# New due times in the first w_in stage, another chain first in the later ones, and separate banks for the last product

## The chip, the cores and the metric

The kernel runs on one core of one Trainium2 chip. The metric is device time in microseconds (us). TensorE is written PE, VectorE DVE, ScalarE ACT, GpSimd POOL, SyncE SP. SBUF is the on-chip memory, PSUM the banks that matrix products are written to. Weights of a product are loaded by a row of their own, PEld.

## The reference

Two operators, one after the other: softmax attention over 8 batches, 12 heads, 448 tokens of 64 elements, and on its result a feed-forward layer with a leaky ReLU.

```python
scores = q @ k.transpose(0, 1, 3, 2) / sqrt(64)
attn = exp(scores - max(scores)); attn = attn / (sum(attn) + 1e-9)
x = (attn @ v).transpose(0, 2, 1, 3).reshape(3584, 768)
h = x @ w_in                      # 768 -> 2048
out = maximum(0.01 * h, h) @ w_out   # 2048 -> 768
```

All inputs and the output are float32; the kernel computes in bfloat16 with float32 sums in PSUM.

## The kernel before

**Units.** Two heads of one batch are a unit; there are 48, in order of batch, and they are written u. For each unit the kernel loads q, k and v (`load_soft`, line 153, by DMAs that POOL issues), casts them (`cast`, line 183, on POOL: L190 for q and k, L198 to L203 for v), transposes q and k (on TensorE as L303 with a VectorE copy L307 for the first 15 units, by SP's DMA afterwards, L276 and L285), computes scores (L321, later L324), exponentials on ScalarE (L333, L336, L338), the weighted sum with v (L364, later L345 and L352), and divides by the row sums on VectorE (a reciprocal L974 and a product L975). The result x is transposed into xT, by SP's DMA or, for three units named in `X_PE`, on TensorE (L391, with a VectorE copy L392).

**Stages.** The tokens are cut into seven stages of 640, 512, 512, 512, 512, 384 and 512. In each stage x is multiplied with w_in, ScalarE applies the leaky ReLU, and the result h is multiplied with w_out; attention for later tokens runs between these products, so that TensorE always has work. Stage 0 is different: its w_in products run in `head` (448 tokens, L426) and `neck` (192 tokens, L814) while w_out is still loading. Stages 1 to 6 use `hidden` for w_in and `second`, which calls `block_pair`, for w_out.

**Seven products for eight.** Both matrix products are split into two halves in three directions and use seven half-size products with sums and differences of operands (Strassen's scheme in Winograd's form). The sums of the weights are made once on VectorE (`mix_w_in`, `mix_weights` with L438, L440, L443, L447, `mix_deep`); those of x and h for each stage (L501, L597, L522 and L523).

**PSUM.** Eight banks are used: two single ones, `banks` (g0, g1), and three pairs, `slots` (sc0 to sc2), each with two banks. In attention a slot takes a pair of scores, a weighted sum, or an x transpose. A bank or slot can be written again when its last reader on ScalarE or VectorE is done.

**w_in stages.** `hidden(i)` works through the hidden columns in two rounds (r) of two groups each. One group's seven products use the two banks, the other's use the first banks of two slots; these are the two chains, `chains = [banks, slots]`. The loop takes one product of each chain in turn, the banks' chain first (x = 0), then the slots' chain (x = 1). Each product is six matmuls (L550). Between rounds the two banks of each chain change places. From stage 2 on a product of the preceding stage's last w_out quarter (`deep`, L646) follows each pair. The stage before ends in `late()` of `block_pair` with a product into each of the two `banks` (L683), read by VectorE in `join` (L694): two reads of the bank b, one of the bank a.

**First stage, planned.** `place` (line 1069) decides in stage 0 what attention work goes between the w_in products. It keeps a model of the time: `model["now"]` for TensorE, `model["act"]` for ScalarE, `free` for the time at which a slot can be written, `ready` for the time at which a unit's exponentials are there, and `owed_x` for x transposes on TensorE, which are due 2.0 after the weighted sum in the model. With `lazy` the last one or two exponentials of a burst of three are emitted later, after the next leaky ReLU (`late`, `settle`). Everything is a fixed order of instructions when the program is built; nothing is decided on the chip.

**POOL's order.** `feed(g)` follows each burst: it casts the next unit (`cast`), then calls `fetch`, which issues loads up to the unit `ahead`. `FAR` is unit 16; from burst 12 on `ahead` is at least FAR.

**The end.** `closing` is the last part of the last stage. One product goes into bank b; ScalarE copies it to the right half of o2 (L733), VectorE adds it to the left half (`join`), and the left half is stored. Then come four products of 192 columns (eight matmuls each, L683): two with the right halves' common operand, into bank a and a slot's bank; VectorE adds each to o2 (L741); and two more that add onto the same two banks, after which VectorE adds the sums to o1. Stores are issued by SP and ScalarE, one part each (L404).

Of the kernel before, what the change touches and what calls it, by code (L numbers as in the profile page):

```python
# [16 lines left out]
def kernel(  # L17
# [9 lines left out]
    nc = tc.nc  # L27
# [6 lines left out]
    NSC = S // SC  # L34
    KD = DM // P
    MD = DF // P
    NW = DM // 2
# [75 lines left out]
    w_out_sb = w_pool.tile([P, MD, DM], BF16)  # L113
# [396 lines left out]
    def token(i, x):  # L510

        return KEEP * P if x == KEEP else cuts[i] + x * P
# [12 lines left out]
    def hidden(i):  # L525

        n = cuts[i + 1] - cuts[i]
        nh = n // 2
        at = place_of(cuts[i])
        near, far = slice(0, KH), slice(KH, KD)  # L530
        one, two = slice(at, at + nh), slice(at + nh, at + n)
        t2, t3, t4 = (x_mix[:, x, :, :nh] for x in range(3))
        hs = h[:, :, spots(i)[0] * P:spots(i)[0] * P + n]
        taken = [next_slot() for _ in range(2)]
        del slots[1:]
        chains = [banks, [x[:, 0] for x in taken]]

        def act(m, cols, x):
            nc.scalar.activation(  # L539
                hs[:, m:m + 2, cols], x.rearrange("p (m t) -> p m t", m=2), AX.Prelu, alpha=0.01  # L540
            )

        def group(chain, m):
            b, a = (x[:, :2 * nh] for x in chain)
            left, right = slice(0, nh), slice(nh, n)

            def product(ps, w, x, first=False):
                for j in range(2):
                    for kk in range(KH):
                        nc.tensor.matmul(  # L550
                            ps[:, j * nh:(j + 1) * nh], w[:, kk, ts(j, P)], x[:, kk],
                            start=(first and j == 0 and kk == 0), stop=(kk == KH - 1), skip_group_check=True,
                        )

            def fresh():
                return c_pool.tile([P, 4 * P], F32, name="c")[:, :2 * nh]

            cl, ch = slice(m * P, (m + 2) * P), slice(FH + m * P, FH + (m + 2) * P)
            s2, s3, s4 = (w_in_mix[:, x, :, cl] for x in range(3))
            product(b, w_in_sb[:, near, cl], xT[:, near, one], first=True)  # L560
            c11 = fresh()
            nc.scalar.copy(c11, b)
            yield
            product(a, w_in_sb[:, far, cl], xT[:, far, one], first=True)
            nc.vector.tensor_add(c11, c11, a)  # L565
            yield
            product(b, s2, t2)
            act(m, left, c11)
            c12 = fresh()
            nc.scalar.copy(c12, b)  # L570
            yield
            product(a, w_in_sb[:, near, ch], xT[:, near, two], first=True)
            c22 = fresh()
            nc.scalar.copy(c22, a)
            yield
            product(b, s3, t3)
            nc.vector.tensor_add(c22, c22, b)
            yield
            product(a, s4, xT[:, far, two])
            nc.vector.tensor_add(c12, c12, a)  # L580
            act(MH + m, right, c22)
            yield
            product(b, w_in_sb[:, far, ch], t4)
            act(m, right, c12)
            act(MH + m, left, b)
            yield

        ready = []
        more = deep(i - 1) if i > 1 else None
        for r in range(2):  # L590
            ms = [4 * r, 4 * r + 2]
            todo = [group(chains[x], ms[x]) for x in range(2)]
            for step in range(7):
                for x in range(2):
                    yield
                    if r == 0 and step == 2 and x:
                        nc.vector.tensor_sub(t4, xT[:, far, one], t2)  # L597
                    next(todo[x])
                    if i > 1 and (r or step) and x == 1:
                        next(more, None)  # L600
                    if step == 2 and ready:
                        mix_h(i, ready.pop(0))
            for c in chains:
                c.reverse()
            ready += ms
        slots.extend(taken)
        for m in ready:
            mix_h(i, m)
# [52 lines left out]
    def block_pair(i, c):  # L661
# [31 lines left out]
        def join(o, at, ps):  # L693
            nc.vector.tensor_add(o[:, at], o[:, at], ps[:, :NW])  # L694
# [34 lines left out]
        def closing():  # L729

            both = (nc.sync, nc.scalar)
            yield from product(b, s3, t3)
            idle(o2[:, right], b[:, :NW])  # L733
            join(o2, left, b)
            store(o2, t0, left, both)
            yield
            pieces = [(ps, ts(x, QW), slice(NW + x * QW, NW + (x + 1) * QW)) for x, ps in enumerate((a, slots[0][:, 0]))]
            for o, y, w, first in ((o2, h[:, lo, two], t1, True), (o1, h[:, hi, one], w_out_sb[:, hi, right], False)):
                for ps, cols, at in pieces:
                    yield from product(ps, y, w[:, :, cols], first=first, cols=cols)  # L740
                    nc.vector.tensor_add(o[:, at], o[:, at], ps[:, cols])  # L741
                    if o is o1:
                        store(o1, token(i, x1), at, both)
                    elif ps is not a:
                        store(o2, t0, right, both)
                    yield

        yield
        if last:
# [208 lines left out]
    def rows():  # L958
        nonlocal rows_done
        u = rows_done  # L960
        ps, n = next_slot(), 2 * (D + 1)
        x_t[u] = x_pool.tile([SC, NSC, 2, D], BF16, name="x")
        if u < HY:
            for j in range(2):
                pairs(u, j, ps[:, j, :NP * n].rearrange("p (q d) -> p q d", q=NSC))
            x = x_t[u].rearrange("p q j d -> p j q d")
        else:
            for qc in range(NSC):
                y, x = divmod(qc, NP)
                weighted(u, qc, ps[:, y, x * n:(x + 1) * n])  # L970
            x = x_t[u].rearrange("p (y q) j d -> p y (q j) d", y=2)
        ps = ps[:SC, :, :NP * n].rearrange("p y (q d) -> p y q d", d=D + 1)
        rec = r_pool.tile([SC, 2, 2 * NP, 1], F32, name="rec2")
        nc.vector.reciprocal(rec, ps[:, :, :, D:])  # L974
        nc.vector.tensor_mul(x, ps[:, :, :, :D], rec.to_broadcast([SC, 2, 2 * NP, D]))  # L975
        if u in X_PE:
            owed_x.append((u, model["now"] + 2.0))
        else:
            x_transposes(u)
        rows_done += 1  # L980
# [58 lines left out]
    def feed(g):  # L1039
        nonlocal ahead  # L1040
        t, r = divmod(g, 4)
        u = 3 * t
        if r < 3:
            if g >= 16:
                ahead = u + 6 + r
            for x, y in enumerate(("q", "cast")):
                if to[y] <= u + 3 + r:
                    cast(u + 3 + r, (x,))
                    to[y] = u + 4 + r
                    fetch(1)  # L1050
            owed_v.append(u + 3 + r)
        elif g == 15:
            cast(NPE, (0, 1))
            to["q"] = to["cast"] = NPE + 1
            dma_transposes(NPE)
            to["turn"] = NPE + 1
        pay()
        if r < 3:
            ahead = max(ahead, u + 5 + r, FAR if g > 11 else 0)
            fetch(6)  # L1060
            load_w({9: 1, 10: 3}.get(g, 0))
        if r > 0 and to["turn"] <= u + 2 + r:
            dma_transposes(u + 2 + r)
            to["turn"] = max(to["turn"], u + 3 + r)
# [4 lines left out]
    def place(i, want, soon=0, full=True, calm=True, first=False, lazy=0, keen=NU, cap=NU):  # L1069
# [3 lines left out]
        while True:  # L1073
# [13 lines left out]
            if want > done and state < 2 and last < NU and not owed_t and turned(last) and rows_done > last - NE and len(slots) == 3 and all(  # L1087
                x <= now + 0.05 + 0.2 * j for j, x in enumerate(at)
            ):
                state = 2  # L1090
                order = list(slots)
                g = chunk // 3
                burst(lazy)
                if first:
                    feed(g)
                done += 1
                for x, t in enumerate(order):
                    model["act"] = max(model["act"], now + 0.45 + 0.2 * x) + 0.8
                    free[id(t)] = model["act"] + (0.3, 0.15 + 0.5 * (lazy > 1), 0.15 + 0.5 * lazy)[x]
                    if old and (3 * g + x) % NSC == KC:  # L1100
                        ready[(3 * g + x) // NSC] = model["act"] + 0.1
                model["now"] = now + 0.78
                continue
            u = to["pe"]
# [138 lines left out]
```

## Time and profile before

| | us |
|---|---|
| median of 3 runs | 380.61 (380.23 to 381.34) |
| profiled execution | 379.86 |
| its span | 378.1 |

| engine | busy us | share |
|---|---|---|
| PE | 370.1 | 98% |
| PEld | 265.5 | 70% |
| ACT | 260.5 | 69% |
| DVE | 254.8 | 67% |
| POOL | 192.5 | 51% |

Busy time by stretch of the span (the first column is the window; then PE, DVE, ACT, POOL):

| window | what runs | PE | DVE | ACT | POOL |
|---|---|---|---|---|---|
| 0 to 24 | attention of the first units | 20.31 | 15.24 | 20.42 | 21.23 |
| 24 to 62 | `head` | 37.47 | 22.62 | 29.30 | 24.30 |
| 62 to 103 | `neck` and w_out of stage 0 | 40.97 | 32.30 | 29.96 | 26.85 |
| 103 to 149 | stage 1 | 46.00 | 32.49 | 33.84 | 37.41 |
| 149 to 197 | stage 2 | 47.94 | 32.59 | 34.01 | 26.75 |
| 335 to 378 | stage 6 | 39.43 | 26.10 | 19.78 | 0.00 |

A line of the timeline has the start in us from the span's start, the time from the first start to the last end of a merged run of instructions, engine and line, operation, out<-in with shapes, the number of instructions, and in brackets the idle time of the engine before it with what ended that. Matmuls are pipelined: the next starts before the end of one is reached, and the ends are modelled. So two runs of matmuls overlap on paper, and a pause is read from the starts.

### The profile page before, as it was taken

To read this page: it belongs to the slowest core of one execution; us is meant where nothing else is said; L and a number is where in the kernel's file an instruction comes from. 1 tells how busy PE (TensorE), PEld (TensorE's weight loads), DVE (VectorE), ACT (ScalarE), POOL (GpSimd) and SP (SyncE) were. 2 spreads that over 40 slices of the span, in tenths; PEclk is the share of its full clock that TensorE was granted. 3 is DMA by queue.
4 is the path that set the end of the run, shared out by engine and by line. 5 is a ranking of instruction groups with operands and counts; after the bars stand their busy time and mean duration, and the time that the engine had idled before them with its cause. 6 is when DMAs were issued, how large, how long until landed. Compare 5 with 4: busy or idle time off the path is not lost.

```text
span 378.1 us, 10135 instructions
## 1 busy us (share of the span) xinstructions
PE 370.1 (98%) x4016; PEld 265.5 (70%) x4016; DVE 254.8 (67%) x557; ACT 260.5 (69%) x399; POOL 192.5 (51%) x377
## 2 busy tenths in 40 slices
PE   7899999999999999999999999999999999999996
PEld 3665657765698556996569966599665995679764
DVE  5763857878666967666587574875847775685763
ACT  6998885766868876658766688666787668636721
POOL 8998641997268996733398234891438020000000
PEclk9999999999999999999999999999999999999999
DMA  9999999999499898964869747698336640321123
GB/s 159 199 200 203 171 193 195 144 145 182 94 182 153 116 133 174 144 142 64 131 140 147 151 64 108 144 147 168 57 65 124 123 109 0 78 58 47 39 54 115
DMA packets 99456, 47.85 MB, mean 127 GB/s; under 512 B 63696, under 2 KB 96208, under 8 KB 99408
## 3 DMA queue, kind: packets, MB, share of 16 engines
q0 software_dynamic: 40384, 22.47, 45.8%
q1 hardware_dynamic: 58576, 24.27, 30.2%
q8 instruction: 31, 0.51, 0.6%
q10 hardware_dynamic: 448, 0.47, 0.4%
q14 instruction: 17, 0.14, 0.1%
HBM read 45.61 MB, written 11.01 MB: 150 GB/s over the span
## 4 chain that ended last, share of the span: by engine, by line
PE 90%; DMA 4%; DVE 2%; ACT 1%; issue 1%; POOL 1%; POOLq 0%; DVEq 0%; ACTq 0%
PE g L683 28%; PE g L550 14%; PE sc L550 14%; PE sc L324 6%; PE sc L352 6%; PE g L426 4%; PE sc L321 4%; PE sc L646 4%; PE sc L364 3%; DMA xT<-x 3%; PE g L814 2%; PE sc L345 2%; DMA w_in_mix<-in_k_dram 2%; PE g L364 1%; PE g L303 1%
## 5 line engine op out<-in xcount | busy, mean ns | idle before, releaser
L333 ACT ACTIVATE e<-sc 128x896 bf16<-128x896 f32 (+1 forms) x144 | 123.6, 922 | 31.8 <-PE sc L324 20.4
L683 PE MATMUL g<-w_out_sb,h 128*128 128x384 bf16 (+1 forms) x448 | 84.9, 324 | 0.1
L683 PEld LDWEIGHTS <-h 128*128 128x128 bf16 x592 | 54.4, 98 | 41.3 <-issue 11.3
L539 ACT ACTIVATE h<-c 128x512 bf16<-128x512 f32 (+1 forms) x72 | 43.6, 611 | 29.4 <-DVE c L565 12.4
L550 PEld LDWEIGHTS <-w_in_sb 128*128 128x128 bf16 x576 | 54.6, 98 | 6.2 <-issue 0.6
L190 POOL COPY qkb<-fq 112x512 bf16<-112x512 bf16 x34 | 23.9, 702 | 47.1 <-DMA qkT<-qkb 38.6
L550 PEld LDWEIGHTS <-w_in_mix 128*128 128x128 bf16 x432 | 40.5, 98 | 3.7
L201 POOL COPY v<-fv 128x384 bf16<-128x384 bf16 x30 | 18.0, 601 | 41.7 <-PE sc L352 38.8
L688 DVE COPY o<-g 128x384 f32<-128x384 f32 x47 | 25.9, 551 | 12.8 <-PE g L683 12.6
L974 DVE RECIPROCAL rec<-sc 112x8 f32<-112x8 f32 x42 | 8.6, 206 | 37.2 <-PE sc L352 16.6
L352 PE MATMUL sc<-v,e 128*128 128x65 bf16 x720 | 33.3, 193 | 0.0
L324 PE MATMUL sc<-qkT 64*128 64x448 bf16 (+1 forms) x210 | 32.8, 352 | 0.0
L352 PEld LDWEIGHTS <-e 128*128 128x128 bf16 x720 | 31.2, 98 | 1.3
L975 DVE TENSOR_TENSOR x<-sc,rec 112x512 bf16<-112x512 f32 x42 | 29.0, 691 | 1.5
L550 PE MATMUL g<-xT,w_in_sb 128*128 128x256 bf16 (+1 forms) x216 | 28.5, 268 | 0.1
L550 PE MATMUL sc<-xT,w_in_sb 128*128 128x256 bf16 (+1 forms) x216 | 28.5, 268 | 0.0
L694 DVE TENSOR_TENSOR o<-o,g 128x384 f32<-128x384 f32 x39 | 21.4, 549 | 8.9 <-PE g L683 4.1
L345 PE MATMUL sc<-v,e 128*128 128x130 bf16 x120 | 26.5, 220 | 0.0
L650 DVE TENSOR_TENSOR o<-o,sc 128x192 f32<-128x192 f32 x39 | 13.7, 351 | 18.3 <-PE sc L646 18.3
L683 PE MATMUL g<-w_mix,h 128*128 128x384 bf16 x128 | 24.6, 326 | 0.0
L163 POOL DMA_DIRECT2D fv<-in_v_dram x32 | 20.1, 643 | 6.7 <-DMA w_out_sb<-in_moe_w_out_dram 3.1
L683 PE MATMUL g<-w_mix,hmix 128*128 128x384 bf16 x112 | 21.7, 326 | 0.0
(151 smaller groups left out, 742.2 us busy)
## 6 DMA issues: line engine op xcount, KB each, us to landing
fq<-in_q_dram POOLq DMA_DIRECT2D x17, 224.0 KB, 5.6
w_in_sb<-in_moe_w_in_dram POOLq DMA_DIRECT2D x4, 768.0 KB, 11.2
w_out_sb<-in_moe_w_out_dram POOLq DMA_DIRECT2D x4, 768.0 KB, 19.1
out_dram<-o SPq DMA_DIRECT2D x7, 336.0 KB, 3.2
out_dram<-o SPq DMA_DIRECT2D x7, 288.0 KB, 3.5
fk<-in_k_dram POOLq DMA_DIRECT2D x15, 128.0 KB, 5.2
fv<-in_v_dram POOLq DMA_DIRECT2D x15, 128.0 KB, 4.8
out_dram<-o SPq DMA_DIRECT2D x7, 240.0 KB, 2.9
```

The costliest lines, as they stand in the source:

```text
L163: nc.gpsimd.dma_start(out=t[p, :n, :, :so].rearrange("p u h so d -> p (u h) (so d)"), in_=(q, k, v)[x][b, hs, keys].rearrange("h (p so) d ...
L190: by(t[:SC, x].rearrange("p so h d -> p h so d"), f)
L324: nc.tensor.matmul(ps[:, j, :S].rearrange("p (so s) -> p so s", so=NSC), t[p, 1, c], t[p, 0, :, :SC], start=True, stop=True,)
L333: nc.scalar.activation(e[:, :, c, :], ps[:n, :, :S], AX.Exp, scale=scale)
L345: nc.tensor.matmul(ps, e[:, EM + qc * SC:EM + qc * SC + P], vt[:, 2 * KC:].rearrange("p j d -> p (j d)"), start=True, stop=False, skip_gro ...
L352: nc.tensor.matmul(ps[:, j * (D + 1):(j + 1) * (D + 1)], e[:, at:at + P], vt[:, j * KC + c], start=False, stop=(c == KC - 1), skip_group_c ...
L539: nc.scalar.activation(hs[:, m:m + 2, cols], x.rearrange("p (m t) -> p m t", m=2), AX.Prelu, alpha=0.01)
L550: nc.tensor.matmul(ps[:, j * nh:(j + 1) * nh], w[:, kk, ts(j, P)], x[:, kk], start=(first and j == 0 and kk == 0), stop=(kk == KH - 1), sk ...
L683: nc.tensor.matmul(ps[:, cols], x[:, m], w[:, m], start=(first and m == 0), stop=(m == MH - 1), skip_group_check=True,)
L688: by(o[:, at], ps[:, :NW])
L694: nc.vector.tensor_add(o[:, at], o[:, at], ps[:, :NW])
L975: nc.vector.tensor_mul(x, ps[:, :, :, :D], rec.to_broadcast([SC, 2, 2 * NP, D]))
```

## The change

Five small edits in three places.

1. In the planner for stage 0: x transposes are due 2.5 instead of 2.0 after the weighted sum; a unit's exponentials count as ready 0.5 later if the last of them belongs to the ones that are emitted late; and the jump to FAR comes one burst later (g > 12 instead of g > 11), so that in burst 12 POOL issues two casts ahead of three loads. What comes out of it: between 53.2 and 61.9 of the span TensorE's instructions stand in another order (three pairs of scores ahead of four x transposes; eight transposes of q and k between two blocks of weighted sums; w_in products in runs of six). On VectorE one L438 moves ahead of an L392, and one L307 ahead of a reciprocal. ScalarE's order follows. Nothing else moves in stage 0, and nothing on SP.
2. In `hidden`, the first of the two rounds takes the slots' chain first and the banks' chain second; the second round is as before. In the list of each engine the two chains' instructions change places in pairs, in stages 1 to 6.
3. In `closing`, `join` stands ahead of ScalarE's copy, so VectorE reads bank b first. The first two products of 192 columns are added to o1 as well as to o2, and the last two go into banks of two other slots, without adding onto the first two. VectorE has six additions of 192 columns instead of four.

```diff
@@ hidden
             for step in range(7):
-                for x in range(2):
+                for y in range(2):
+                    x = y if r else 1 - y
                     yield
-                    if r == 0 and step == 2 and x:
+                    if r == 0 and step == 2 and y:
                         nc.vector.tensor_sub(t4, xT[:, far, one], t2)
                     next(todo[x])
-                    if i > 1 and (r or step) and x == 1:
+                    if i > 1 and (r or step) and y == 1:
                         next(more, None)
@@ closing
             yield from product(b, s3, t3)
+            join(o2, left, b)
             idle(o2[:, right], b[:, :NW])
-            join(o2, left, b)
             store(o2, t0, left, both)
             yield
-            pieces = [(ps, ts(x, QW), slice(NW + x * QW, NW + (x + 1) * QW)) for x, ps in enumerate((a, slots[0][:, 0]))]
-            for o, y, w, first in ((o2, h[:, lo, two], t1, True), (o1, h[:, hi, one], w_out_sb[:, hi, right], False)):
-                for ps, cols, at in pieces:
-                    yield from product(ps, y, w[:, :, cols], first=first, cols=cols)
+            cuts2 = [(ts(x, QW), slice(NW + x * QW, NW + (x + 1) * QW)) for x in range(2)]
+            for (cols, at), ps, os in zip(cuts2, (a, slots[0][:, 0]), ((o1, o2), (o2, o1))):
+                yield from product(ps, h[:, lo, two], t1[:, :, cols], first=True, cols=cols)
+                for o in os:
                     nc.vector.tensor_add(o[:, at], o[:, at], ps[:, cols])
-                    if o is o1:
-                        store(o1, token(i, x1), at, both)
-                    elif ps is not a:
-                        store(o2, t0, right, both)
-                    yield
+                if ps is not a:
+                    store(o2, t0, right, both)
+                yield
+            for (cols, at), slot in zip(cuts2, slots[1:]):
+                ps = slot[:, 0]
+                yield from product(ps, h[:, hi, one], w_out_sb[:, hi, right][:, :, cols], first=True, cols=cols)
+                nc.vector.tensor_add(o1[:, at], o1[:, at], ps[:, cols])
+                store(o1, token(i, x1), at, both)
+                yield
@@ rows
-            owed_x.append((u, model["now"] + 2.0))
+            owed_x.append((u, model["now"] + 2.5))
@@ feed
-            ahead = max(ahead, u + 5 + r, FAR if g > 11 else 0)
+            ahead = max(ahead, u + 5 + r, FAR if g > 12 else 0)
@@ place
-                        ready[(3 * g + x) // NSC] = model["act"] + 0.1
+                        ready[(3 * g + x) // NSC] = model["act"] + 0.1 + 0.5 * (lazy and x > 2 - lazy)
```

## The prediction

> **What bounds the kernel now.** I read the page first, then the timeline wherever the change touches it. Times are of the profiled execution: 379.86 us, a span of 378.1 and 1.76 around it. It lies 0.75 under the median of 380.61.
>
> ```profile
> PE 370.1 (98%) x4016; PEld 265.5 (70%) x4016; DVE 254.8 (67%) x557; ACT 260.5 (69%) x399; POOL 192.5 (51%) x377
> ...
> PEclk9999999999999999999999999999999999999999
> ...
> PE 90%; DMA 4%; DVE 2%; ACT 1%; issue 1%; POOL 1%; POOLq 0%; DVEq 0%; ACTq 0%
> ```
>
> TensorE is busy 98% of the span, its granted clock is full in all slices, and 90% of the chain that ended last is TensorE's. The change leaves the matmuls as many as they are, so only TensorE's pauses can move. Matmul ends are modelled and overlap the next start, so I read pauses from starts: the same block with and without a wait. First stage, end of the w_in products:
>
> ```profile
> 53.23 0.56 PE L303 MATMUL g<-ident,qkb 112*128 112x112 bf16 x8
> 53.92 0.37 PE L391 MATMUL sc<-ident,x 112*128 112x112 bf16 x4
> 54.13 0.73 PE L426 MATMUL g<-xT,w_in_sb 128*128 128x448 bf16 x3
> 54.79 0.92 PE L321 MATMUL sc<-qkT 64*128 64x448 bf16 x6
> ...
> 59.23 0.36 PE L391 MATMUL sc<-ident,x 112*128 112x112 bf16 x4
> ```
>
> Eight L303 transposes take 0.39 undisturbed (29.23 to 29.62); here L391 follows after 0.69, because L975 on VectorE makes x until 53.17+0.69 = 53.86. Six L321 take 0.67 (34.48 to 35.15); here 0.85 (L426 follows at 55.64). The second block of 32 L364 begins near 57.82 (56.79 plus the 1.03 of one block) and ends at 59.23, after 1.41, because ScalarE's exponentials in c (L336) run 57.30 to 58.23. These pauses sum to 0.30+0.18+0.38 = 0.86.
>
> ```profile
> 65.03 0.56 DVE L438 TENSOR_TENSOR w_mix<-w_out_sb 128x768 bf16<-128x768 bf16 x1 [0.48 <-DMA w_out_sb<-in_moe_w_out_dram]
> ...
> 73.28 0.62 DVE L307 COPY qkT<-sc 128x896 bf16<-128x896 bf16 x1
> ```
>
> VectorE is idle for 0.48 until w_out's last quarter lands, then works without a gap from 65.03 to 74.39. Inside stands L307, ending at 73.90; it makes the qkT of unit 14, which the scores of L321 need: six of them start at 73.76, and the second pair (0.20 a pair, so 73.96) reads it. TensorE arrives there with nothing to spare.
>
> ```profile
> 147.68 1.46 PE L683 MATMUL g<-w_out_sb,h 128*128 128x384 bf16 x8
> ...
> 148.62 1.12 DVE L694 TENSOR_TENSOR o<-o,g 128x384 f32<-128x384 f32 x2
> ...
> 149.21 0.81 PE L550 MATMUL g<-xT,w_in_sb 128*128 128x256 bf16 x6
> ```
>
> Start of stage 2. From the last w_out product to the first w_in product pass 1.53; where nothing waits it is 1.30 (101.91 to 103.21, 292.38 to 293.68, 334.12 to 335.42). The first of the two L694 still reads the bank that L550 writes. Stages 3 and 4 pay 0.11 each (195.99 to 197.40, 244.19 to 245.60).
>
> ```profile
> 371.47 0.82 PE L683 MATMUL g<-w_out_sb,h 128*128 128x192 bf16 x8
> 372.13 0.82 PE L683 MATMUL sc<-w_out_sb,h 128*128 128x192 bf16 x8
> 373.05 0.82 PE L683 MATMUL g<-w_out_sb,h 128*128 128x192 bf16 x8
> 373.71 0.82 PE L683 MATMUL sc<-w_out_sb,h 128*128 128x192 bf16 x8
> ```
>
> The end. The four half-width products start 0.66 apart, but the third 0.92 after the second: it adds onto the bank that VectorE's first L741 reads from 372.65 to 373.00. That L741 is late because the join ahead of it (L694, 372.18 to 372.74) waited for ScalarE's copy L733 of the same bank, 371.67 to 372.15. The last L741 starts at 374.57.
>
> **The change part by part.**
>
> **(1) First stage.** The planner's new due times reorder TensorE from 53.23 to 61.92: scores before the x transposes, unit 13's transposes between the two L364 blocks, fewer switches. Laid out from the rows: L303 0.49 (0.10 for the switch to scores), L321 0.67, six L426 1.14, L391 0.21 reach 55.74; L364 waits for the second exponential of the scores, 54.10+1.73, so 55.89 to 56.92; L303 0.39; L364 1.03 to 58.34 (c is ready near 57.1); L391 0.21, L426 1.14 to 59.69; L391 waits for VectorE to 59.8; then L426 to 61.13. L814 began at 61.92, so 0.79 less. VectorE's L438 now stands ahead of L392: an xT copy, two reciprocals and their products queue behind the w_out landing of 56.25, and the transposes of 58.34 wait for the first product, done near 58.2; a later landing up to the 0.79 costs nothing at 73.96.
>
> POOL runs unit 13's two casts (1.17) ahead of three loads. They move from 57.24 to about 49.9; the q load moves from 49.81 to about 51.0, and nothing needs it before the cast at 75.06. The k and v loads keep their times, since they wait at 52.75 and 56.55 for landings. SP's queue is as it was. I price the casts at nothing; without that cover it is at most their 1.17.
>
> Where does the 0.79 go? Up to 73.76 nothing stands in its way, but the second score pair waits for L307. VectorE is in order and full since 65.03, and that start is set by a landing, not by TensorE. So TensorE arrives near 73.2 and waits until 73.96. **Part 1 is worth 0**; its ends are 0, if the landing stays, and 0.79, if it comes that much sooner. Landings in the rows come in the order of issue: w_out's last quarter, issued at 40.40, ends a wait at 65.03, the q load of 46.83 one at 66.00, so moving a q load issued at 49.8 should not reach the quarter. If they shared bandwidth instead, the moved 224 KB at the 193 GB/s of that slice are 1.2 us, enough for the full 0.79. The Trainium skill (DMA: Bandwidth & Descriptors, Two DMAs through the same engine are not ordered) says that descriptors of one queue on one engine start in order; the two landings agree. By that rule part 1 gives 0, by shared bandwidth 0.79. The same page (Queues, rings and completion order) lets other queues interleave by packets, but SP's transfers are not moved here.
>
> **(2) w_in stages.** In the first round the slots' chain goes ahead of the banks' chain. The first product writes a slot whose exponentials ended early (stage 2: 144.68+2.53 = 147.21, needed at 148.98), and the bank's product comes 0.65 later, after L694's end at 149.16. Saved: 0.23+0.11+0.11 = **0.45**; stages 1, 5 and 6 had no wait and save 0. What is late next is the turn of the rounds, where the banks' chain stays first in the second round and loses one product, 0.65, of its distance: stage 1 writes at 115.69 a bank whose last ScalarE read, now fourth in line, ends at 114.94+0.59 = 115.53; stage 2 at 162.00 against 161.18. Both hold, so 0; if ScalarE's line were 1.2 later, about 1.1 in stage 1 and 0.4 in each other stage. VectorE's adds change order only between the chains and end by 113.97 for a bank written at 114.38. Ends for this part: 0 and 0.45.
>
> **(3) The end.** The join goes ahead of ScalarE's copy, and the last two products get banks of their own. The join runs 371.67 to 372.23, the copy 372.26 to 372.74, which holds back ScalarE's first store as now (372.77). Two more L741 of 0.35 appear: o1 at 372.33, o2 from 372.78, then two more to about 373.7. The third product needs no wait and starts at 372.79, the fourth at 373.45, ending at 374.27; its add starts at 374.31 instead of 374.57, and the last stores on SP and ScalarE go 0.26 sooner. Saved: **0.26**; ends 0, if VectorE's six adds become the limit, and 0.35, one add.
>
> Sum: 0+0.45+0.26 = 0.71. 379.86-0.71 = 379.15 for a profiled execution; on the median, 380.61-0.71 = **379.9**.
>
> **The rivals.** *B, part 1 survives:* the w_out quarter lands sooner or VectorE's run shortens; for it, VectorE's 0.96 rows (66.10, 69.34, 71.45) beside 0.56 for the same form show slack in that run; against it, the order of landings. 0.71+0.79 = 1.50, 379.1. *C, the change does little:* another wait takes the bank's place at the stage starts (for it: VectorE also has three L501 there until 150.88; against: they end before the products that read them), leaving 0.26: 380.35. *D, slower:* the turn of the rounds. If ScalarE runs 1.2 later there, two L539, the six stages lose 1.1+5x0.4 = 3.1, net 2.4: 383.0. It decides once ScalarE is more than 0.8 later than I place it; against it, ScalarE is idle 1.20 and 1.14 before its activations in stage 2 (157.15, 163.65), and only stage 1 is tight.
>
> **How the numbers follow.** About 0.3% (1.14 us) is what a measurement of this kernel can tell from no change: under 379.47 is faster, over 381.75 slower. Chances: main case 0.48 (its own range 379.4 to 380.4), B 0.30, C 0.12, D 0.10. Faster: 0.17 of the main case and 0.85 of B, 0.08+0.26 = 0.34. Slower: 0.9 of D, 0.09. Same: 0.57. The range 378.9 to 380.6 takes in B, the main case and most of C; it leaves out D above and about 0.08 at the two ends.
>
> **What would show it.** Right: L814 begins near 61.1; L303 near 71.8; the second score pair still starts near 73.96 behind L307; L683 to L550 take 1.30 at every stage start; the last four products are 0.66 apart. Wrong: L307 ends near 73.1 (B); a pause near 115.7 or 162 (D); a new wait ahead of the first slot product (C); the q cast of 75.06 later.

## The result, and the profile after

The changed kernel took 378.93 us in the median of ten runs (378.29 to 379.92), the kernel before 380.31 beside it: a ratio of 0.9963, 95% interval 0.995 to 0.9976, 1.38 us less. Two later measurements beside the kernel before gave 0.9989 (0.9974 to 1.0004) and 0.9968 (0.9946 to 0.999). The mean of the three is 0.9973, about 1.0 us. The first measurement is past the bound of 0.3% given in the prediction, the mean just short of it. The profiled execution took 378.71 us, with a span of 376.9.

The page of the changed kernel, engine line, granted clock and chain:

```profile
PE 368.8 (98%) x4016; PEld 265.4 (70%) x4016; DVE 255.6 (68%) x559; ACT 260.4 (69%) x399; POOL 191.5 (51%) x377
...
PEclk9999999999999999999999999999999999999999
...
PE 95%; DMA 2%; DVE 1%; ACT 1%; issue 1%; POOL 0%; POOLq 0%; ACTq 0%
```

The clock is full as before, and TensorE's share of the chain went from 90% to 95%: less of the path is waiting. From here on I use an *offset*: the start of a matmul in one trace minus the start of the same matmul, counted along TensorE, in the trace of before. It begins at +0.49, which arises before 11 us, while the first units' loads come in and both kernels do the same; only later steps of the offset count.

The timeline of the changed kernel, first stage (columns as before: start, length, engine, line, operation):

```profile
53.73 0.56 PE L303 MATMUL g<-ident,qkb 112*128 112x112 bf16 x8
54.22 0.74 PE L321 MATMUL sc<-qkT 64*128 64x448 bf16 x6
...
57.48 0.55 PE L303 MATMUL g<-ident,qkb 112*128 112x112 bf16 x8
...
58.91 0.36 PE L391 MATMUL sc<-ident,x 112*128 112x112 bf16 x4
...
61.57 1.15 PE L819 MATMUL g<-xT,w_in_sb 128*128 128x192 bf16 x12
```

L303 is 0.50 later than before (53.23), L819 (L814 before, at 61.92) 0.35 earlier: the stage lost 0.85.

```profile
65.23 0.56 DVE L438 TENSOR_TENSOR w_mix<-w_out_sb 128x768 bf16<-128x768 bf16 x1 [1.53 <-DMA w_out_sb<-in_moe_w_out_dram]
...
72.94 0.62 DVE L307 COPY qkT<-sc 128x896 bf16<-128x896 bf16 x1
...
73.42 0.74 PE L321 MATMUL sc<-qkT 64*128 64x448 bf16 x6
```

L307 ends at 73.56, and the second score pair (0.20 after 73.42) needs it at 73.62. The offset stays at -0.34 from 67 to 77 us: TensorE did not wait there.

Start of stage 2, then the end:

```profile
147.13 1.46 PE L684 MATMUL g<-w_out_sb,h 128*128 128x384 bf16 x8
...
148.43 0.82 PE L550 MATMUL sc<-xT,w_in_sb 128*128 128x256 bf16 x6
```

```profile
371.13 2.14 PE L684 MATMUL sc<-w_out_sb,h 128*128 128x192 bf16 x24
...
373.32 0.35 DVE L749 TENSOR_TENSOR e<-e,sc 128x192 f32<-128x192 f32 x1 [0.31 <-PE sc L684]
```

148.43 - 147.13 is 1.30 (1.53 before), and stages 3 and 4 have 1.30 too. The last 24 matmuls, three products, run without a gap: 0.66 apart each.

### The profile page after: what moved, and what is told of

The parts are those of the page before. It is cut to its first block, busy times and chain, and to the rows that moved or that the text cites. A ratio compares the mean times of both kernels' runs of the same rounds, so it can differ in the third digit from the quotient of the medians.

```text
span 376.9 us, 10134 instructions
## 1 busy us (share of the span) xinstructions
PE 368.8 (98%) x4016; PEld 265.4 (70%) x4016; DVE 255.6 (68%) x559; ACT 260.4 (69%) x399; POOL 191.5 (51%) x377
## 4 chain that ended last, share of the span: by engine, by line
PE 95%; DMA 2%; DVE 1%; ACT 1%; issue 1%; POOL 0%; POOLq 0%; ACTq 0%
PE g L684 30%; PE g L550 14%; PE sc L550 14%; PE sc L324 7%; PE sc L352 6%; PE g L426 4%; PE sc L321 4%; PE sc L647 4%; PE sc L364 3%; PE g L819 2%; PE sc L345 2%; DMA w_in_mix<-in_q_dram 2%; PE g L303 1%; PE g L364 1%; PE sc L426 1%; DVE qkb L190 1%
## 5 line engine op out<-in xcount | busy, mean ns | idle before, releaser
L550 PEld LDWEIGHTS <-w_in_sb 128*128 128x128 bf16 x576 | 54.6, 98 | 5.7
L190 POOL COPY qkb<-fq 112x512 bf16<-112x512 bf16 x34 | 22.6, 664 | 47.3 <-DMA qkT<-qkb 37.8
L550 PEld LDWEIGHTS <-w_in_mix 128*128 128x128 bf16 x432 | 40.6, 98 | 3.7
L201 POOL COPY v<-fv 128x384 bf16<-128x384 bf16 x30 | 18.8, 626 | 42.3 <-PE sc L352 39.7
L689 DVE COPY o<-g 128x384 f32<-128x384 f32 x47 | 25.9, 552 | 12.9 <-PE g L684 12.9
L550 PE MATMUL g<-xT,w_in_sb 128*128 128x256 bf16 (+1 forms) x216 | 28.5, 268 | 0.0
L550 PE MATMUL sc<-xT,w_in_sb 128*128 128x256 bf16 (+1 forms) x216 | 28.5, 268 | 0.0
L695 DVE TENSOR_TENSOR o<-o,g 128x384 f32<-128x384 f32 x39 | 21.4, 549 | 9.1 <-PE g L684 4.3
```

Source lines behind the costliest of these rows:

```text
L190: by(t[:SC, x].rearrange("p so h d -> p h so d"), f)
L550: nc.tensor.matmul(ps[:, j * nh:(j + 1) * nh], w[:, kk, ts(j, P)], x[:, kk], start=(first and j == 0 and kk == 0), stop=(kk == KH - 1), sk ...
L689: by(o[:, at], ps[:, :NW])
```

## The experiments

The parts alone first. L975, L694 and so on keep the numbers of the kernel that a trace is from.

**Part 1 alone** (`e1_planner`):

```diff
-            owed_x.append((u, model["now"] + 2.0))
+            owed_x.append((u, model["now"] + 2.5))
-            ahead = max(ahead, u + 5 + r, FAR if g > 11 else 0)
+            ahead = max(ahead, u + 5 + r, FAR if g > 12 else 0)
-                        ready[(3 * g + x) // NSC] = model["act"] + 0.1
+                        ready[(3 * g + x) // NSC] = model["act"] + 0.1 + 0.5 * (lazy and x > 2 - lazy)
```

> Part 1 alone: the planner's three numbers (2.5, g > 12, the later ready time), nothing of the w_in stages or the end. Theory A (the prediction's): the first stage gets shorter by 0.79 up to about 73 us, and then TensorE waits for L307 at the second score pair, so the time stays within 0.1 us of the kernel before (ratio 1.000). Theory B: VectorE's run ahead of L307 gets shorter too, or its end was no limit, and the time falls by about 0.8 us (ratio 0.9979). In the trace: by A the step from TensorE's offset against the kernel before, gained near 61, is gone again after the second score pair; by B it is still there in stage 2.

Measured: 0.9993 (0.9982 to 1.0005); 380.17 against 380.14. The time looks like theory A, the trace does not:

```profile
72.67 0.62 DVE L307 COPY qkT<-sc 128x896 bf16<-128x896 bf16 x1 [0.45 <-PE sc L303]
...
73.15 0.74 PE L321 MATMUL sc<-qkT 64*128 64x448 bf16 x6
...
146.25 0.43 DVE L501 TENSOR_TENSOR x_mix<-xT 128x512 bf16<-128x512 bf16 x1 [1.61 <-DMA xT<-x]
...
148.92 0.82 PE L550 MATMUL g<-xT,w_in_sb 128*128 128x256 bf16 x6 [0.26 <-DVE o L694]
```

The offset falls by 0.84 (from +0.23 to -0.61) and stays at -0.61 past 77 us. Ahead of L307 it is VectorE that waits 0.45, for TensorE's transposes. So in this execution nothing was swallowed at the score pair. What it lost, it lost at stage 2: L501 waited for x's transposing transfer, the copies and L694 stood behind it, and TensorE took 0.58 more than its 2.60 for the last two w_out products. But at 379.43 this is also the shortest execution of the eleven. Its trace shows that part 1's gain can last; it does not explain why the median is no lower than before, and the interval leaves out theory B's 0.9979 too. The time of part 1 alone stays unexplained.

**Part 2 alone** (`e2_slots_first`):

```diff
-                for x in range(2):
+                for y in range(2):
+                    x = y if r else 1 - y
```

(and y for x in the two conditions below it).

> Part 2 alone: in the first round of each w_in stage the slots' chain goes first. Prediction: 0.23 + 0.11 + 0.11 = 0.45 us less, all of it at the starts of stages 2, 3 and 4 (ratio 0.9988). Rival C: another wait takes the bank's place and nothing is gained (1.000). Rival D: TensorE waits near 115.7 or 162 at the turn of the rounds and the time rises by up to 2.4 us (1.006).

Measured: 0.9996 (0.9985 to 1.0007). From the last w_out product to L550 pass 1.30 at all six starts, as forecast, and there is no pause at the turns of the rounds. But one product earlier stands another wait:

```profile
147.48 0.42 DVE L501 TENSOR_TENSOR x_mix<-xT 128x512 bf16<-128x512 bf16 x1 [1.80 <-DMA xT<-x]
147.83 0.55 DVE L689 COPY o<-g 128x384 f32<-128x384 f32 x1
...
148.43 1.46 PE L684 MATMUL g<-w_out_sb,h 128*128 128x384 bf16 x8 [0.43 <-DVE o L689]
```

x landed late, L501 held up L689 behind it, and L689 held the bank that the last w_out product writes: 0.60 lost. Part 2 moves the w_in products; it cannot help a w_out product.

**Part 3 alone** (`e3_end`), the whole edit of `closing`, which is shown above:

> Part 3 alone: the join ahead of ScalarE's copy, and banks of their own for the last two products. Prediction: 0.26 us less (ratio 0.9993), the third product 0.66 after the second instead of 0.92. Rival: VectorE's two more adds of 0.35 become the limit and nothing is gained (1.000).

Measured: 0.9991 (0.9978 to 1.0003), and in the trace 0.66 for 0.92 at the third product, 0.26 less. As forecast. This kernel has no part 2, and yet:

```profile
147.54 1.46 PE L683 MATMUL g<-w_out_sb,h 128*128 128x384 bf16 x8
148.84 0.82 PE L550 MATMUL g<-xT,w_in_sb 128*128 128x256 bf16 x6
```

1.30 at stage 2 without part 2: in this execution L501 began at 145.06 without waiting for x, and the bank was free in time.

**The L447s behind L307** (`e4_late_L447`), on the changed kernel:

```diff
-            for _ in range((3, 4, 2, 2, 1, 0, 0, 0)[x]):
+            for _ in range((3, 4, 2, 1, 0, 0, 0, 0)[x]):
-                    if x in (1, 6):
+                    if x in (1, 3, 6, 8):
```

> The changed kernel, with two of the four L447 taken from ahead of L307 to behind it: VectorE's run from w_out's landing to L307 loses about 1.5 to 1.9 us, and all else stays. If L307 holds TensorE at the second score pair (theory A), this kernel gains what part 1 loses there: up to 0.8 us less than the changed kernel, 378.1 (ratio 0.994). If L307 is in time anyway in the changed kernel (theory B), it makes no difference: 378.9 (ratio 0.9963). Between the two: its late end costs only a part, as the trace of the changed kernel has 0.06 us between L307's end and the score pair that reads it, in an execution whose first stage began 0.49 us late.

Measured: 0.9984 (0.9972 to 0.9996), 379.54. It gained nothing over the changed kernel (378.93 in the first measurement), so theory A's gain did not come. The kernel was not only that, though: its trace shows part 1's gain lost in quite another place.

```profile
58.10 0.56 DVE L438 TENSOR_TENSOR w_mix<-w_out_sb 128x768 bf16<-128x768 bf16 x1 [2.43 <-DMA w_out_sb<-in_moe_w_out_dram]
...
59.11 0.69 DVE L980 TENSOR_TENSOR x<-sc,rec 112x512 bf16<-112x512 f32 x1
...
59.85 0.37 PE L391 MATMUL sc<-ident,x 112*128 112x112 bf16 x4 [0.61 <-DVE x L980]
```

Part 1 put L438 ahead of an L392 and of the products that make x. w_out's third landing came at 58.10 here (57.03 in the changed kernel's first trace), so x was late and TensorE waited; the stage gained 0.02 for 0.85. Later the offset grows by 0.35 near 78 and 0.59 near 87. The L447s that now stand there may be the cause of the first; a wait like the second appears in `e9_casts_behind` too, where they are not moved. At 380.89 the profiled execution is also the longest of the eleven. So the run of VectorE ahead of L307 was not tested cleanly by this kernel.

**Three more on the changed kernel, and the kernel itself again.** One edit puts L438 behind the L392s (`e6_L438_back`):

```diff
-                for _ in range({13: 1, 15: 2}.get(m, 0)):
+                for _ in range({15: 2}.get(m, 0)):
-            for _ in range((3, 4, 2, 2, 1, 0, 0, 0)[x]):
+            for _ in range((4, 4, 2, 2, 1, 0, 0, 0)[x]):
```

and one puts the L501s later (`e7_x_later`); `e8_both` has both:

```diff
-                        fresh[y] = model["now"] + (5.0 if i + 2 == NR else 6.0 if i else 7.0)
+                        fresh[y] = model["now"] + (5.0 if i + 2 == NR else 8.0 if i else 7.0)
```

> The changed kernel once more, unedited, beside the next three. The prediction's sum is 0.71 us (ratio 0.9981); the first measurement gave 0.9963 with an interval of 0.995 to 0.9976; the three parts alone gave 0.26, 0.15 and 0.34 us by their ratios, 0.75 together (0.998). Theory L (landings): the parts' worth hangs on when two transfers land in each execution, so the ratio lies between 0.9963 and 0.998 again and the time varies by about 1.5 us from run to run. Theory S (parts help each other: 1.38 together, 0.75 alone): 0.9963 again.

> The changed kernel with one edit: on VectorE, the L438 that waits for w_out's third landing goes behind the second and third L392 and the reciprocals, products and L307 between, instead of ahead of them. In the traces so far it landed at 56.25 to 58.10 us, and at 58.10 TensorE waited 0.61 us at its x transposes (L391 at 59.85) and part 1's gain was gone. Theory L: part 1's gain no longer hangs on that landing, and the median falls by 0.2 to 0.5 us against the changed kernel; in the trace L391 follows the second L364 block without a pause, whatever the landing. Theory A (the gain is swallowed later, at the score pair that waits for L307): no change in the time.

> The changed kernel with one edit: the L501 at the end of stages 1 to 4 count x as ready 8 us after its rows instead of 6, which puts the first L501 behind two more L689 and an L695 on VectorE. In the traces so far stage 2's first L501 began between 145.06 and 148.41 after waiting for x's transposing transfer, with the copies that free the products' banks queued behind it, and from the last w_out product but one to the first w_in product TensorE lost 0 to 0.61 us there with and without part 2. Theory L: 0.1 to 0.5 us less than the changed kernel, none of it lost at stage 2 in the trace. Rival: the L501s now end too late for the products of stage 2 that read them, and the time stays or rises by up to 1 us.

> The changed kernel with the edits of the last two together. Theory L: the sum of both, 0.3 to 1.0 us less than the changed kernel, and a narrower spread from run to run. Theory A: only the second one's part.

Measured, in one comparison:

| kernel | median us | ratio | interval |
|---|---|---|---|
| e5_changed_again | 379.24 | 0.9989 | 0.9974 to 1.0004 |
| e6_L438_back | 378.80 | 0.997 | 0.9956 to 0.9984 |
| e7_x_later | 380.61 | 1.0016 | 1.0 to 1.0031 |
| e8_both | 380.39 | 1.0014 | 0.9999 to 1.0028 |

The unedited kernel came out nearer to the kernel before (0.9989) than either theory had it. `e6_L438_back` lies 0.44 below it, as theory L said; `e8_both`, forecast 0.3 to 1.0 below it, lies 1.15 above.

`e6_L438_back` did what it should in the trace:

```profile
56.54 0.39 DVE L392 COPY xT<-sc 128x448 bf16<-128x448 bf16 x1 [1.01 <-ACT e L333]
...
58.94 0.36 PE L391 MATMUL sc<-ident,x 112*128 112x112 bf16 x4
...
61.18 0.55 DVE L438 TENSOR_TENSOR w_mix<-w_out_sb 128x768 bf16<-128x768 bf16 x1
```

No landing stands ahead of x any more, and L438 itself finds its data. `e7_x_later` went as its rival said. Stage 2 of its trace:

```profile
148.10 0.42 DVE L501 TENSOR_TENSOR x_mix<-xT 128x512 bf16<-128x512 bf16 x1
...
151.04 0.47 DVE L501 TENSOR_TENSOR x_mix<-xT 128x256 bf16<-128x256 bf16 x1
151.44 0.67 DVE L565 TENSOR_TENSOR c<-c,sc 128x512 f32<-128x512 f32 x1
...
152.63 0.34 DVE L651 TENSOR_TENSOR o<-o,sc 128x192 f32<-128x192 f32 x1
...
153.02 0.49 PE L647 MATMUL sc<-w_mix,h 128*128 128x192 bf16 x4 [0.20 <-DVE o L651]
```

The copies now come first but wait for TensorE, the L501s slip behind them, everything after them on VectorE is late, and TensorE pays 0.50 in stage 2 (offset -0.94 to -0.44), 0.51 in stage 3 and 0.50 in stage 4: 1.51, of the size of the 1.37 between 380.61 and 379.24. In the trace of `e8_both` the offset rises at the same three places, by 0.85, 0.51 and 0.50.

**POOL's casts back behind the loads** (`e9_casts_behind`). In the built program this edit of part 1 moves only POOL's instructions; the later `ready` moves none, so the 2.5 alone makes the order of TensorE and VectorE.

```diff
-            ahead = max(ahead, u + 5 + r, FAR if g > 12 else 0)
+            ahead = max(ahead, u + 5 + r, FAR if g > 11 else 0)
```

> The changed kernel with one edit of part 1 undone (g > 11 again): on POOL, unit 13's two casts stand behind the q, k and v loads as in the kernel before; TensorE's, VectorE's, ScalarE's and SP's orders are those of the changed kernel. The v load waits for a landing of w_out, and ended at 57.2 to 57.9 us in most traces; the casts then run to about 58.4 to 59, and TensorE's transposes of unit 13, which began at 57.22 to 57.66 in the traces with part 1, begin 1.0 to 1.3 us later. So part 1 without this edit should lose its 0.84 and some more: 0.9 to 1.3 us above the changed kernel (ratio about 1.001 against the kernel before). The prediction priced the casts at nothing where they are moved and at up to 1.17 without that cover. Rival: the scheduler's edit is idle, since the transposes could wait without harm: no difference.

Measured: 1.0038 (1.0012 to 1.0063), 381.54 beside 378.99 of the changed kernel: slower than before, and with a wide spread (380.07 to 384.67).

```profile
56.40 0.70 POOL L163 DMA_DIRECT2D fv<-in_v_dram  x1 [3.06 <-DMA w_out_sb<-in_moe_w_out_dram]
57.10 1.17 POOL L190 COPY qkb<-deep_mix 112x512 bf16<-112x512 bf16 x2
```

```profile
57.77 0.37 PE L303 MATMUL g<-ident,qkb 112*128 112x112 bf16 x4 [0.47 <-POOL qkb L190]
58.32 0.37 PE L303 MATMUL g<-ident,qkb 112*128 112x112 bf16 x4 [0.18 <-POOL qkb L190]
```

The v load waits on POOL for w_out, the casts for the load, the transposes for the casts. From 53.43 to 63.40 the offset rises by 0.15 where it otherwise falls by 0.85: 1.00 lost, as expected. The rest of the 2.5 is not explained by this wait in the one execution that was profiled; against the third trace of the changed kernel it loses another 0.49 near 87, 0.31 near 128 and 0.64 at stage 2, and kernels with the casts ahead have lost such amounts at the first and last of these places too. Part of the 2.5 goes with the clock: six of the twelve runs show a granted clock of 0.991 to 0.996 and took 381.95 to 384.67; the six others, at 0.999 or more, took 380.07 to 381.12, with a median of 380.38. That is 1.43 above the 378.95 of the changed kernel's eleven runs at 0.998 or more. Why half of the runs had the lower clock, no run shows.

**Last comparison:** `e11_L438_again` and `e12_changed_third` repeat; `e10_L438_and_one_L689` is the L438 edit with 6.4 in place of the 8.0 above, so that one L689 goes ahead of the first L501.

> The kernel with L438 behind the L392s, and the L501s counted ready 6.4 us after their rows instead of 6: at the end of stages 1 to 4 one L689 goes ahead of the first L501 and the second L689 and an L695 ahead of the third. Theory L: the wait for that L689 (0, 0.09, 0.16, 0.52 and 0.60 us in the traces so far) is gone whatever x's landing is, and the products of the next stage that read the L501s are no later than before, unlike with 8 us, where they were 0.32 us late at 153.02: 0.1 to 0.3 us less than with L438 moved alone. Rival: VectorE idles for TensorE ahead of that L689, as it did with 8 us, and the L501s end too late again: up to 1.4 us more.

> The kernel with L438 behind the L392s once more. Theory L: again 0.2 to 0.5 us below the changed kernel beside it, ratio 0.996 to 0.998 against the kernel before. Rival: the 0.44 us between the two in the last comparison were scatter, and they stand even.

> The changed kernel a third time, beside the others. The two measurements so far gave 0.9963 and 0.9989; the prediction's sum of 0.71 us is 0.9981. Expected between the two, 0.997 to 0.9985.

Measured: 378.86 us, 0.9961 (0.9939 to 0.9982); 378.84, 0.9968 (0.9948 to 0.9987); 378.99, 0.9968 (0.9946 to 0.999). L438 moved back was 0.44 below the changed kernel in one comparison and 0.15 in the other; the intervals overlap in both, so a gain is likely and not shown. `e10_L438_and_one_L689` gained nothing over L438 moved alone, where 0.1 to 0.3 was forecast; the 0.15 of `e11_L438_again` falls short of its 0.2 to 0.5; the changed kernel's 0.9968 is just past its 0.997 to 0.9985. In `e10_L438_and_one_L689` no wait is left at stage 2, and VectorE's wait for TensorE did no harm this time:

```profile
146.19 0.56 DVE L689 COPY o<-g 128x384 f32<-128x384 f32 x1 [1.31 <-PE g L684]
146.66 0.41 DVE L501 TENSOR_TENSOR x_mix<-xT 128x512 bf16<-128x512 bf16 x1
```

It has the lowest ratio of all, but it is not told apart from the other two either.

**All traces side by side.** *Start* is the offset at 25 us, *part 1* its change from before's 53.43 to 63.40, *idle* VectorE's wait for TensorE ahead of the L307 near 73; *copy* is what the last w_out product ahead of stage 2 lost waiting for L689 (L688), *bank* what the first w_in product lost at stages 2, 3 and 4; *end* is the start of the third narrow product after the second. us.

| trace | start | part 1 | idle | copy | bank | end |
|---|---|---|---|---|---|---|
| before | 0 | 0 | 0 | 0 | 0.23, 0.11, 0.11 | 0.92 |
| changed | 0.49 | -0.85 | 0 | 0 | 0, 0, 0 | 0.66 |
| e1_planner | 0.23 | -0.84 | 0.45 | 0.16 | 0.42, 0, 0 | 0.92 |
| e2_slots_first | 0.22 | 0 | 0.45 | 0.60 | 0, 0, 0 | 0.92 |
| e3_end | -0.04 | 0 | 0.45 | 0 | 0, 0.11, 0 | 0.66 |
| e4_late_L447 | 0.67 | -0.02 | 0.45 | 0.09 | 0, 0, 0 | 0.66 |
| e5_changed_again | 1.04 | -0.84 | 0.45 | 0 | 0, 0, 0 | 0.66 |
| e6_L438_back | 0.53 | -0.84 | 0 | 0.52 | 0, 0, 0 | 0.66 |
| e7_x_later | 0.14 | -0.84 | 0.45 | 0 | 0, 0, 0 | 0.66 |
| e8_both | 0.43 | -0.84 | 0 | 0 | 0, 0, 0 | 0.66 |
| e9_casts_behind | 0.16 | +0.15 | 0.45 | 0.64 | 0, 0, 0 | 0.66 |
| e10_L438_and_one_L689 | 0.33 | -0.85 | 0.45 | 0 | 0, 0, 0 | 0.66 |
| e11_L438_again | 1.61 | -0.85 | 0.45 | 0 | 0, 0, 0 | 0.66 |
| e12_changed_third | 0.33 | -0.85 | 0.22 | 0 | 0, 0, 0 | 0.66 |

The trace of before is an early starter: only one of the others is earlier, and eight of the thirteen start 0.33 or more later. That can be part of the 0.75 by which it lies under its median in the prediction; the rest is not explained. The table has one execution of each kernel, and the changed kernel's own three (changed, `e5_changed_again`, `e12_changed_third`) differ in start and idle.

## Why the prediction was right or wrong

The time of 379.9 was 0.97 above the first measurement, which lies 0.03 above the low end of the range; the likeliest case, a gain too small to tell from no change, was not what that measurement gave. Of the 0.97, 0.30 is the kernel before, which took 380.31 beside it instead of 380.61. That the range held is owed to rival B, which it took in; for the sum's own working it is luck. In the traces rival B is what happened: part 1's gain lasts, and L307 ends at 73.56, which, less the late start of 0.50, is the 73.1 that the prediction named as B's sign. The medians alone do not decide it: 1.38, 0.62 and 1.15 less, 1.05 on average, lie between the sum's 0.71 and B's 1.50.

- **Part 1, the local saving.** Forecast 0.79, measured 0.84 to 0.85 in nine of the ten traces that have both the new order and the casts ahead. L819 came at 61.57 with a start 0.50 late (forecast 61.1), the second L303 at 72.27 (forecast 71.8): both right. The layout writes 54.10+1.73 as 55.89, which is 55.83; nothing hangs on the 0.06.
- **Part 1, "worth 0": the step that failed.** "VectorE is in order and full since 65.03, and that start is set by a landing, not by TensorE. So TensorE arrives near 73.2 and waits until 73.96." In no trace did TensorE wait there longer than in the trace of before: from the first of the eight L303 ahead of L307 to the second score pair pass 1.34 in all fourteen. L307 copies what these L303 write, and it begins 0.66 to 0.67 after the first of them, in the trace of before too:

```profile
72.61 0.56 PE L303 MATMUL sc<-ident,qkb 112*128 112x112 bf16 x8
...
73.28 0.62 DVE L307 COPY qkT<-sc 128x896 bf16<-128x896 bf16 x1
```

So TensorE's own transposes set that start; VectorE's run, with L975 done at 73.25, only came to the same place at the same time, and the 0.03 between is too short to be printed. The run would have become the limit only if it had not moved. But it was full in that one execution; in nine of the other thirteen traces VectorE idles 0.45 ahead of L307, waiting for TensorE, and in one 0.22 (in `e4_late_L447`, one of the nine, the run was shortened by an edit). Nor has the run a fixed length: from the L438 behind the landing to the end of the last L447 ahead of L307 the same ten operations took 6.84 to 7.38 in the thirteen traces that have them, and 6.84, 6.85 and 7.28 in the changed kernel's own three. In its first trace the run began at 65.23, later than before, and was 0.54 shorter. `e2_slots_first` and `e3_end` show it with TensorE's old order of the first stage: there L438 began at 64.82 and 64.43 instead of 65.03. I had taken the landing for fixed and the run for rigid, from one trace, although the prediction itself listed the 0.96 rows as slack. The right reading of those rows was that a chain of this make has a spread of half a microsecond. In three of the ten traces with the change's order (changed, `e6_L438_back`, `e8_both`) no idle time is left ahead of L307, so the gain has little to spare there.
- **The landing rule.** By shared bandwidth, moving the q load would have brought w_out's last quarter 1.2 sooner; by the order of issue, not at all. The quarter landed at 63.85 to 65.48 in the ten traces with the q load moved, 64.58 on average, and at 64.94, 64.72, 63.77 and 63.71 in the four with it in its old place (before, e2, e3, e9), 64.29 on average; from issue to landing passed 23.62 and 23.54. So it did not land sooner, and the gain did not come from it. The Trainium skill (DMA: Bandwidth & Descriptors, Two DMAs through the same engine are not ordered) says that descriptors within one queue of one engine start in order; these landings agree.
- **L438 ahead of L392.** I wrote that a later landing costs nothing because the time is lost at 73.96 anyway. Without that later loss it costs in full: at 58.10 in `e4_late_L447` TensorE idles 0.61 for x, and 0.83 of the stage's 0.85 is gone. It may be part of why the three medians stay below the 1.44 that the traces add up to (0.85 of part 1, 0.33 of part 2 as priced below, 0.26 of part 3). It cannot be all: only this one of the six traces with L438 and POOL's casts ahead lost anything there, and with L438 moved the gain over the kernel before is 1.06 and 1.30, still short of 1.44. The rest stays open; the wait for L689, the last point of this list, is another candidate.
- **POOL's casts.** Priced at nothing where they were moved, and at 1.17 without. `e9_casts_behind` lost 1.00 at that place in the trace. Right, and more important than it looked: the new order of TensorE needs them. The later q cast, named as a danger, came at 75.60 instead of 75.06, hardly more than this execution's late start, and nothing waited for it.
- **Part 2.** 0.45 in the changed kernel's first trace (0.23, 0.11, 0.11), as forecast, and 0 of bank wait in every trace that has part 2. But the price was that of one execution: the kernels without it lost 0.45, 0.42 and 0.11, so 0.33 on average. The prediction took L694 as fixed in place; it stands behind L501, which waits for x's transfer. Rival D, a wait at the turn of the rounds, came in no trace.
- **Part 3.** 0.26 forecast, 0.26 in every trace that has it.
- **Not forecast:** the wait of the last w_out product for L689, 0 to 0.64, which comes and goes in kernels with and without the change.

## What to carry over

A wait on a landing is a draw, not a number. Before a gain is written off because "the next wait takes it", or a wait is priced, ask what starts the chain behind it, and look at what the waiting instruction itself reads: an engine that shows no idle time need not be the one that holds it up. If a DMA starts the chain, look whether the waiting instruction stands in an in-order queue ahead of work that the critical engine needs, and move it behind that work. When single traces disagree by more than the effect, compare the starts of the same instructions along the bounding engine; steps of that difference show what a change did, even where the medians scatter. Say then where the profiled execution's own time lies among its kernel's: the one of `e1_planner` was the shortest of eleven, and its trace does not explain the median.

## What the runs showed of the hardware

A VectorE operation on two bfloat16 tensors in SBUF mostly took about twice as long here when it began while one of POOL's copies was running. Before, then changed:

```profile
66.00 0.65 POOL L190 COPY qkb<-fq 112x512 bf16<-112x512 bf16 x1 [7.59 <-DMA fq<-in_q_dram]
...
66.10 0.96 DVE L438 TENSOR_TENSOR w_mix<-w_out_sb 128x768 bf16<-128x768 bf16 x1
```

```profile
66.30 0.55 DVE L438 TENSOR_TENSOR w_mix<-w_out_sb 128x768 bf16<-128x768 bf16 x1
...
66.52 0.80 POOL L190 COPY qkb<-fq 112x512 bf16<-112x512 bf16 x1 [8.62 <-PE g L819]
```

The same L438 takes 0.96 when POOL's copy began 0.10 ahead of it, and 0.55 when it began 0.22 ahead of the copy, which then took 0.80 for 0.65. In all fourteen traces, of the operations of 128x768 (L438, L440, L443, L447) between 55 and 82 us, 63 of the 78 that began during a copy took more than 0.75, and 14 of the other 15 met only its last 0.08; of 122 with no copy in their first 0.5, all but two took 0.54 to 0.67. The Trainium skill (SBUF — State Buffer, Who interferes with whom) says that a VectorE instruction with two SBUF inputs contends with a GpSimd instruction that reads SBUF, over a port held by an exclusive lock, and that the order of issue decides who blocks. The rows agree on who pays, less well on how much: by an estimate from them, a lock held to the end of the first instruction would have made L438's 0.96 a 1.10, and the copy's 0.80 a 0.98. In `e4_late_L447` and `e9_casts_behind` an L523 beside a cast took 1.17, where it took 0.47 in the changed kernel, and the bank that its successor L695 frees came 0.56 late for TensorE. So a shift of a few tenths between the two engines changes which of them pays, and with it the length of VectorE's run ahead of L307. No run here changes that alone.
